# A gated mix of attention and a state-space convolution, forward and backward: a new order of work inside the channel loop

## The chip, the cores and the metric

The kernel runs on one core of one Trainium2 chip. The metric is the device time of one execution in microseconds (us). Three runs of the kernel before took 2802.67, 2806.47 and 2811.53 us; the median is 2806.47 us. A separate execution was recorded by the hardware profiler.

## The reference

The program computes a function and all its gradients (a vector-Jacobian product with a given output gradient):

```python
x = A_x                                                     # 1 x 2048 x 576, bf16
g = sigmoid((x * gate_w).sum(-1, keepdims=True))
a = attention(x, wqkv, wo)                                  # 32 heads of 18, softmax
b = s4_convolution(x, A, B, C, log_dt) + x * Dskip          # per channel, by FFT
return g * a + (1 - g) * b
```

The convolution kernel of a channel d is `K[d, l] = Re sum_n C[d,n] exp(dt_d A[d,n] l) dt_d B[d,n]`, with 128 complex states n, over the length 2048. Its outputs are the value itself and the gradients with respect to x, the attention weights, the complex parameters A, B and C, `log_dt`, `Dskip` and `gate_w`.

## The kernel before

The program has four stages, one after the other: projections and parameter preparation; attention forward and backward (most of the time); the channel loop, which does the convolution and its gradients; and a last stage with the weight gradients and the output projections. The change lies in the channel loop alone, between about 2147 and 2630 us of the profiled span.

The loop doesn't use an FFT. The 2048 positions are cut into 16 chunks of 128. Within a chunk the convolution is a 128 x 128 Toeplitz matrix for each channel (`T0w`), across chunks a recurrence runs over the 128 states. The 576 channels are taken in 18 blocks of 32 (`NBLK`, `CB`). A block passes through these steps; the engine that does it stands behind each:

- `load_en`: loads the table of powers of the exponential, `E1n`, in two halves h of 16 channels, 1 MB each (sync queue). `load_par`: three loads with 12 rows of parameters, `par` (sync). `load_rx`: the two input sequences, `RXn`, for a pair of blocks (sync).
- `prep_rx`: rearranges `RXn` into `RX`, channel by channel, and scales two copies (one copy and two multiplications of ScalarE; lines 598 to 600).
- `m_load`, `m_part`, `m_skw`, `m_sum`, `m_fin`: the gradient of the kernel at short lags. Shifted tokens `xs` and `gyp` are loaded (sync), 32 small matmuls make products in PSUM (TensorE), ScalarE copies them to `mst`, two stores put them into DRAM (`Md_d`), four loads read them back along the diagonals (`skw`), and `m_sum` adds them by eight matmuls into a column range of the PSUM tile `misc`. `m_fin` copies the result to `RX` and to a row of gradients (ScalarE). These rows are what the title's "short lags" are.
- `turn_e`: turns one half of `E1n` by 32 TensorE transposes, which four ScalarE copies bring to `E1e`.
- `uv`: 32 matmuls of `E1e` with `RX`, taken out of PSUM by four ScalarE operations to `UV`.
- `scan_open`, `scan`: the recurrence over chunks on VectorE, on `HG`, with the parameters `par`. The second half of block i's chunks and the first half of block i+1's are run together.
- `rw1`, `rw2`: VectorE makes the weighted states `Rw`. `casts`: ScalarE casts the states to bf16 (`hR`, `gR`) and copies two columns to `CK`.
- `k0`: ScalarE casts a parameter row (`wk`), 65 small matmuls make the kernel's first 128 lags in `misc`, ScalarE copies them (`K0c`), and a store writes them to DRAM (`Kp_d`). `t0_load`: reads them back as the Toeplitz matrices `T0w`, 1 MB; it waits for that store.
- `t0`: 32 matmuls of `T0w` with `RX` into the PSUM tile `yp`. `ybp`: 64 matmuls of `E1n` with `Rw` add to `yp`; ScalarE copies the sum to `yd`, and for each second block a store follows.
- `pairs1`, `pairs2`: VectorE multiplies pairs of states; 59 matmuls with the identity (`psum`) add them up in `misc`. `sums`: ScalarE copies them (`m4`, shown as `m`), GpSimd combines them into `SS`.

All PSUM results of `m_part`, `turn_e` and `uv` share four buffers (tag `bk`), `misc` has two tiles that alternate by block, and most other tiles have one or two buffers. The order on all five engines in this loop is written out by hand (`tc.manual_schedule`): each engine executes its instructions in the order in which the program text issues them. A load or a store is an instruction of the queue that issues it, so what it waits for also holds what stands behind it. In iteration i the loop works on block i (the end of its scan, `t0`, `ybp`, the pairs), on `i + 1` (first scan half, `k0`, `t0_load`), on `sb = i + 2` (`prep_rx`, `m_sum`, `turn_e`, `uv`, `load_par`) and on `mb = i + 3` (`m_part`, `load_en`, `m_skw`). Before the loop, `Md_d` and `skw` go through the sync queue; within it, through GpSimd's queue:

```python
Q["mdma"] = nc.gpsimd.dma_start
```

Of the kernel before, what the change touches and what calls it, by code (L numbers as in the profile page):

```python
# [11 lines left out]
BF = mybir.dt.bfloat16  # L12
# [5 lines left out]
P = 128  # L18


def build(tc, aps, dbg_aps=None, stages=("s1", "attn", "post", "s4", "final")):
    nc = tc.nc
# [6 lines left out]
    def mm(out, lhsT, rhs, start=True, stop=True, **kw):  # L29
        return nc.tensor.matmul(out, lhsT=lhsT, rhs=rhs, start=start, stop=stop, **kw)  # L30
# [31 lines left out]
    with ExitStack() as gctx:  # L62
# [27 lines left out]
        NS = NB - 1  # L90
# [11 lines left out]
        CB = 32  # L102
# [481 lines left out]
        def load_rx(xb, dma=nc.sync.dma_start):  # L584
            d0 = xb * XB
            RXn = Q["pl"].tile([P, 2 * NB, XB], BF, tag="RXn", bufs=1, name="RXn")
            dma(RXn[:, 0:NB, :], xr_d[:, :, d0:d0 + XB])
            dma(RXn[:, NB:2 * NB, :], gyr_d[:, :, d0:d0 + XB])
            RXs[xb] = [RXn, None]
# [88 lines left out]
        def load_en(b, h, dma=nc.sync.dma_start, pieces=1):  # L678
            dG = b * CB + h * GS
            En = blk(b)["En"][h] = Q["en", (2 * b + h) % 6 // 2].tile([P, GS, 2, P], BF, tag="E1n", bufs=2, name="E1n")  # L680
            n = GS // pieces

            def piece(x):
                dma(En[:, x * n:(x + 1) * n], E_d[:, dG + x * n:dG + (x + 1) * n])
            piece(0)
            return piece
# [45 lines left out]
                    t0v, t1v = [tz[x][:, m].rearrange("p (r s) c -> p r s c", r=2) for m in range(2)]  # L732
                    nc.vector.tensor_tensor(HG[:, :, k, :].rearrange("p (r s) c -> p r s c", r=2), t0v, t1v[:, ::-1], op=A.add)

        def casts(b):
            B_ = blk(b)
            HGv = B_["HG"].rearrange("p (r s) k c -> p r s k c", s=2)
            for nm, s_ in (("hR", 0), ("gR", 1)):
                B_[nm] = Q["pw"].tile([P, 2, NS, CB], BF, tag=nm, name=nm)
                nc.scalar.copy(B_[nm], HGv[:, :, s_, ::-1, :])  # L740
            B_["Rw"] = Q["pw"].tile([P, 2, 2 * NS, CB], BF, tag="Rw", name="Rw")
            nc.scalar.copy(Q["CK"][:, :, :, b * CB:(b + 1) * CB], B_["UV"][:, :, CDK:CDK + 2, :])

        def rw1(b):
            B_ = blk(b)
# [5 lines left out]
        def rw2(b):  # L751
# [2 lines left out]
            nc.vector.tensor_tensor(Rw[:, 0], wb[:, 2 * NS:], wa[:, 0:2 * NS], op=A.subtract)  # L754
            nc.vector.scalar_tensor_tensor(Rw[:, 1], wa[:, 2 * NS:], -1.0, wb[:, 0:2 * NS], op0=A.mult, op1=A.subtract)

        def k0(b):

            B_ = blk(b)
            wk = Q["pw"].tile([P, 2, CB], BF, tag="wk", bufs=2, name="wk")  # L760
            nc.scalar.copy(wk, B_["par"][:, 10:12, :])
            kps = Q["misc2"][b % 2][:, 13 * CB:14 * CB]
            mm(kps, lhsT=ident_bf[0:1, :], rhs=Q["dsk_row"][:, b * CB:(b + 1) * CB], start=True, stop=False)
            for ch in range(CB):
                for ri in range(2):
                    mm(kps[:, ch:ch + 1], lhsT=B_["En"][ch // GS][:, ch % GS, ri, :], rhs=wk[:, ri, ch:ch + 1],
                       start=False, stop=(ch == CB - 1 and ri == 1))
            K0c = Q["pw"].tile([P, CB], BF, tag="K0c", bufs=2, name="K0c")
            nc.scalar.copy(K0c, kps)
            nc.sync.dma_start(Kp_d[b, P:2 * P, :], K0c)  # L770

        def t0(b, h):
            B_ = blk(b)
            RX = RXs[b // 2][1]
            T0w = B_["T0w"]
            yp = B_["yp", h] = Q["ps"].tile([P, 2, NB, GS], F32, tag="yp", bufs=2, name="yp")
            for c_ in range(GS):
                mm(yp[:, :, :, c_].rearrange("p a b -> p (a b)"), lhsT=T0w[:, :, h * GS + c_],
                   rhs=RX[:, (b % 2) * CB + h * GS + c_, 0:2 * NB], start=(c_ == 0), stop=False)

        def ybp(b, h):
            B_ = blk(b)
            Rw, En = B_["Rw"].rearrange("p r (s k) c -> p r s k c", s=2), B_["En"].pop(h)
            yp = B_.pop(("yp", h))
            for c_ in range(GS):
                ch = h * GS + c_
                for ri in range(2):
                    mm(yp[:, :, 1:, c_], lhsT=En[:, c_, ri, :], rhs=Rw[:, ri, :, :, ch], start=False, stop=(c_ == GS - 1 and ri == 1))
            if h == 0 and b % 2 == 0:
                ydx[b // 2] = Q["pw"].tile([P, 2, NB, XB], BF, tag="yd", name="yd")  # L790
            yd = ydx[b // 2]
            o0 = (b % 2) * CB + h * GS
            nc.scalar.copy(yd[:, :, :, o0:o0 + GS], yp)
            if h == 1 and b % 2 == 1:
                x0 = (b // 2) * XB
                (act_dma if b == NBLK - 1 else nc.sync.dma_start)(yd_d.rearrange("p a b d -> p (a b) d")[:, :, x0:x0 + XB], yd.rearrange("p a b d -> p (a b) d"))
# [41 lines left out]
        def t0_load(b):  # L838
            B_ = blk(b)
            if "T0w" in B_:  # L840
                return
            T0w = B_["T0w"] = Q["pw"].tile([P, P, CB], BF, tag="T0w", bufs=1, name="T0w")
            src = bass.AP(tensor=Kp_d.tensor, offset=Kp_d[b:b + 1, 1:2, 0:1].offset, ap=[[CB, P], [1, P * CB]])
            nc.sync.dma_start(T0w.rearrange("p j c -> p (j c)"), src)
# [487 lines left out]
        if "s4" in stages:  # L1332
# [8 lines left out]
            with ExitStack() as ctx:  # L1341
# [26 lines left out]
                with tc.manual_schedule(engines={mybir.EngineType.SP}):  # L1368
                    prep_rx(0, dve_copy)
                    load_en(2, 0)  # L1370
                    k0(0)
                    t0_load(0)
                    turn_e(0, 0, 0, 4, dve_copy)
                    m_sum(0)
                    m_fin(0)
                    uv(0, 0)
                    prep_rx(1, dve_copy)
                    load_rx(1)
                    turn_e(0, 1, 0, 4, dve_copy)
                    m_part(1, 0)  # L1380
                    m_part(1, 1)
                    m_skw(1)
                    m_load(2)
                    uv(0, 1)
                    turn_e(1, 0, 0, 4, dve_copy)
                    scan_open(0)
                    scan((0, 1, KH, 0), (0, 1, KH, 1))
                    turn_e(1, 1, 0, 4)
                    m_sum(1)
                    m_fin(1)  # L1390
                    load_en(2, 1)
                    uv(1, 0)
                    m_part(2, 0)
                    m_part(2, 1)
                    m_skw(2)
                    uv(1, 1)
                    m_load(3)
                    Q["mdma"] = nc.gpsimd.dma_start
                    for i in range(NBLK):
                        nx = i + 1 < NBLK  # L1400
                        mb = i + 3 if i + 3 < NBLK else None
                        sb = i + 2 if i + 2 < NBLK else None
                        if nx:
                            scan_open(i + 1)
                            scan((i, KH, NS, None), (i + 1, 1, KH, None))
                        else:
                            scan((i, KH, NS, 0), (i, KH, NS, 1))
                        t0(i, 0)
                        t0(i, 1)
                        if nx:  # L1410
                            k0(i + 1)
                            t0_load(i + 1)
                        if sb is not None:
                            prep_rx(sb)
                            m_sum(sb)
                            m_fin(sb)
                            if sb % 2 == 1 and sb + 1 < NBLK:
                                load_rx((sb + 1) // 2)
                            turn_e(sb, 0, 0, 4)
                            uv(sb, 0)  # L1420
                        casts(i)
                        rw1(i)
                        rw2(i)
                        if mb is not None:
                            m_part(mb, 0)
                            m_part(mb, 1)
                            if mb + 1 < NBLK:
                                m_load(mb + 1)
                        if sb is not None:
                            load_par(sb)  # L1430
                            turn_e(sb, 1, 0, 4)
                            uv(sb, 1)
                        ybp(i, 0)
                        if mb is not None:
                            load_en(mb, 0)
                        ybp(i, 1)
                        if mb is not None:
                            load_en(mb, 1)
                            m_skw(mb)
                        pairs1(i)  # L1440
                        pairs2(i)
                        sums(i)
                        BK.pop(i)

# [297 lines left out]
```

## Time and profile before

| | |
|---|---|
| median of three runs | 2806.47 us (2802.67 to 2811.53) |
| the profiled execution's own time | 2811.18 us |
| its span in the profile | 2809.5 us |
| granted TensorE clock, mean over the span | 0.945 |
| first scan of the loop (line 708, iteration 0) | 2147.72 us |
| scan of iteration 1 | 2169.41 us |
| scan of iteration 2 | 2197.57 us |
| last of these (iteration 16) | 2591.9 us |
| DMA issues per iteration | sync queue 10 to 11, GpSimd's queue 6 |

The profile names engines PE (TensorE matmul), PEld (TensorE weight load), DVE (VectorE), ACT (ScalarE), POOL (GpSimd) and SP (the sync queue; SPq is its issuing of DMAs). A row of waits says which engine's instruction at which line stood idle until which other work ended, with the total in us, the number of times and the longest. A row of the timeline gives the start in us, the duration, the engine, the line and the operation with output and inputs; in square brackets stands the idle time before it and what ended it. Line 30 is the helper that issues every matmul, so matmuls are told apart by their tiles. "DMA share" is the sum of the durations of all DMA packets over the time of 16 engines; it can exceed 1, since packets overlap.

### The profile page before, as it was taken

The numbers are of one execution on the slowest core, as the hardware profiler recorded it, in microseconds if no ns is written. First come the engines' busy times: TensorE is split into PE (matmuls) and PEld (weight loads), VectorE is DVE, ScalarE is ACT, GpSimd is POOL, SyncE is SP. The second block draws the span as 40 slices with busy tenths as digits, with TensorE's granted clock in tenths as the row PEclk, the third lists the DMA queues.
The fourth block names the chain that finished last, engine by engine and source line by source line (L and its number), as shares of the span: only waits on it lengthen the run. The fifth ranks groups of instructions, "written<-read, shape, count | busy, mean of one in ns | idle before, by whom it ended". The sixth has DMA issues, their size and how long they took to land. (4 is left out here: it accounts for less than half of the span.)

```text
span 2809.5 us, 70096 instructions
## 1 busy us (share of the span) xinstructions
PE 2473.9 (88%) x27411; PEld 1180.0 (42%) x27411; DVE 2301.7 (82%) x4141; ACT 2356.0 (84%) x2744; POOL 1790.9 (64%) x2757
## 2 busy tenths in 40 slices
PE   8898989999889899998998989988877888888789
PEld 4433333333333333333333333333326787878557
DVE  4649999999989989999999989998866877787945
ACT  5479999999999999999999999999845777777111
POOL 0278878887888888788888888878111444443110
PEclk9879999999999999999999999999858888988899
DMA  7637899889889988977988998896698787875996
GB/s 222 179 94 160 153 173 174 161 156 189 159 161 171 168 162 164 178 161 156 186 156 159 173 168 154 164 178 140 128 201 216 198 220 205 221 204 154 251 247 143
DMA packets 1249559, 492.00 MB, mean 175 GB/s; under 512 B 1163205, under 2 KB 1216566, under 8 KB 1240522
## 3 DMA queue, kind: packets, MB, share of 16 engines
q1 hardware_dynamic: 1207466, 402.18, 71.1%
q0 software_dynamic: 28400, 72.58, 10.1%
q10 hardware_dynamic: 13360, 12.75, 1.6%
q8 instruction: 215, 3.52, 0.5%
q14 instruction: 118, 0.97, 0.1%
HBM read 146.86 MB, written 98.52 MB: 87 GB/s over the span
## 5 line engine op out<-in xcount | busy, mean ns | idle before, releaser
L1311 DVE TENSOR_TENSOR ds<-ps_P,PT 128x512 bf16<-128x512 f32 x2048 | 1312.1, 683 | 127.4 <-PE ps_P L30 87.8
L1306 ACT ACTIVATE eb<-ps_P 128x1024 bf16<-128x1024 f32 x1024 | 1101.0, 1075 | 40.0 <-PE ps_P L30 39.9
L1301 ACT ACTIVATE PT<-ps_P 128x1024 bf16<-128x1024 f32 x1024 | 1106.1, 1081 | 25.8 <-PE ps_P L30 24.7
L30 PE MATMUL ps_P<-dOaT,VaT_g 32*128 32x512 bf16 x2048 | 582.3, 390 | 29.5 <-DVE ds L1311 14.5
L502 POOL TENSOR_TENSOR et<-eG,eT 128x448 f32<-128x448 f32 x576 | 542.2, 961 | 10.7
L30 PE MATMUL ps_P<-QaT_g,KaT_g 32*128 32x512 bf16 x2048 | 404.9, 387 | 137.9 <-ACT PT L1301 124.4
L30 PE MATMUL ps_P<-KaT_g,QaT_g 32*128 32x512 bf16 x2048 | 408.3, 391 | 1.2 <-ACT eb L1306 0.6
L30 PEld LDWEIGHTS <-KaT_g 32*128 32x128 bf16 x2048 | 147.7, 91 | 467.4 <-issue 452.0
L502 POOL TENSOR_TENSOR Eo<-et,et 128x448 bf16<-128x448 f32 x288 | 326.8, 1135 | 20.8
L30 PEld LDWEIGHTS <-QaT_g 32*128 32x128 bf16 x2048 | 116.5, 91 | 287.0 <-issue 264.7
L30 PE MATMUL accV<-eb,dOa 128*32 128x512 bf16 x2048 | 186.8, 398 | 27.5 <-ACT eb L1306 27.3
L30 PE MATMUL accO<-PT,Vtok_g 128*32 128x512 bf16 x2048 | 207.7, 395 | 0.1
L30 PE MATMUL accK<-dsT,Qtok_g 128*32 128x256 bf16 x4096 | 164.0, 282 | 17.0 <-DMA dsT<-ds 15.2
L30 PE MATMUL accQ<-ds,Ktok_g 128*32 128x512 bf16 x2048 | 161.2, 393 | 2.1 <-DVE dvacc L1069 2.0
L30 PEld LDWEIGHTS <-Vtok_g 128*32 128x32 bf16 x2048 | 52.8, 93 | 223.1 <-issue 223.1
L835 POOL TENSOR_TENSOR SS<-m 128x96 f32<-128x96 f32 x18 | 100.0, 5557 | 69.4 <-ACT m L833 69.4
L1020 DVE COPY dsT<-turn_p 128x1024 bf16<-128x1024 bf16 (+1 forms) x216 | 139.1, 644 | 2.1 <-PE turn_p L1015 2.1
L1015 PE MATMUL turn_p<-ident_bf,ds 128*128 128x128 bf16 x1664 | 134.6, 224 | 1.6 <-DVE gb L1087 0.8
L30 PE MATMUL uvp<-RX,E1e 128*128 128x64 bf16 x1152 | 94.3, 260 | 40.9 <-ACT E1e L666 37.8
L666 ACT COPY E1e<-etp 128x1024 bf16<-128x1024 bf16 x132 | 127.3, 1124 | 1.5 <-PE etp L665 1.5
L502 POOL TENSOR_TENSOR et<-eT 128x32 f32<-128x32 f32 (+3 forms) x288 | 115.9, 422 | 11.4
L30 PEld LDWEIGHTS <-Qtok_g 128*32 128x32 bf16 x4096 | 88.3, 97 | 81.6 <-issue 59.8
(270 smaller groups left out, 3754.6 us busy)
## 6 DMA issues: line engine op xcount, KB each, us to landing
E_d<-Eo POOLq DMA_DIRECT2D x144, 256.0 KB, 3.4
E1n<-E_d SPq DMA_DIRECT2D x32, 1024.0 KB
xs<-xb_d SPq DMA_DIRECT2D x18, 1024.0 KB
T0w<-Kp_d SPq DMA_DIRECT2D x18, 1024.0 KB
Md_d<-mst POOLq DMA_DIRECT2D x30, 288.0 KB, 7.6
dsT<-ds SPq DMA_TRANSPOSE x512
dqkv_d<-dtk POOLq DMA_DIRECT2D x96, 72.0 KB, 4.4
KaT_g<-QKV_d SPq DMA_DIRECT2D x32, 128.0 KB
```

What stands on the lines that cost most here:

```text
L30: return nc.tensor.matmul(out, lhsT=lhsT, rhs=rhs, start=start, stop=stop, **kw)
L502: nc.gpsimd.tensor_tensor(out, a, b, op=op)
L666: copy(E_[:, 4 * q:4 * q + 4], pt_)
L835: nc.gpsimd.tensor_tensor(o_[:, :, 0], m4[:, :, 0], m4[:, :, 3], op=A.subtract)
L1015: nc.tensor.transpose(pt_[:, x, qb, :], t_[:, qb * P:(qb + 1) * P], ident_bf)
L1020: (nc.scalar.copy if NTOT <= now[0] < NTOT + OFF else nc.vector.tensor_copy)(o_(), pt_[:, x:x + n])
L1301: nc.scalar.activation(U["PT"][i, j // 2], ps, ACT.Exp)
L1306: nc.scalar.activation(e, ps, ACT.Exp)
L1311: nc.vector.tensor_tensor(U["ds"][i][:, j, :], ps, U["PT"][i, j // 2][:, j % 2, :], op=A.mult)
```

## The change

The loop's order within an iteration is rewritten. Three helpers are split so that their parts can stand apart: `casts` into `cast1` (called once for `hR`, once for `gR`), `rw2_open` and a bare copy to `CK`; `k0` into `wk_cast`, `k0` and `k0_out`; `ybp` into the matmuls and `yd_out`. `m_sum` and `m_part` now begin TensorE's iteration; `k0` follows the first `turn_e`; `t0` follows the first `uv`; the second `uv` stands between the two halves of `ybp`. `prep_rx` is done for block `mb`, one iteration earlier than before, beside the second half of `ybp`, with `prep_rx(2)` and `wk_cast(1)` ahead of the loop. `wk_cast` comes at the end of the iteration before its use. VectorE's order is as it was. The line that sends `Md_d` and `skw` to GpSimd's queue is gone, so these six DMAs stay on the sync queue in the loop.

```diff
-        def casts(b):
+        def cast1(b, nm, s_):
             B_ = blk(b)
             HGv = B_["HG"].rearrange("p (r s) k c -> p r s k c", s=2)
-            for nm, s_ in (("hR", 0), ("gR", 1)):
-                B_[nm] = Q["pw"].tile([P, 2, NS, CB], BF, tag=nm, name=nm)
-                nc.scalar.copy(B_[nm], HGv[:, :, s_, ::-1, :])
-            B_["Rw"] = Q["pw"].tile([P, 2, 2 * NS, CB], BF, tag="Rw", name="Rw")
-            nc.scalar.copy(Q["CK"][:, :, :, b * CB:(b + 1) * CB], B_["UV"][:, :, CDK:CDK + 2, :])
+            B_[nm] = Q["pw"].tile([P, 2, NS, CB], BF, tag=nm, name=nm)
+            nc.scalar.copy(B_[nm], HGv[:, :, s_, ::-1, :])
+
+        def rw2_open(b):
+            blk(b)["Rw"] = Q["pw"].tile([P, 2, 2 * NS, CB], BF, tag="Rw", name="Rw")
...
+        def wk_cast(b):
+            wk = blk(b)["wk"] = Q["pw"].tile([P, 2, CB], BF, tag="wk", bufs=2, name="wk")
+            nc.scalar.copy(wk, blk(b)["par"][:, 10:12, :])
+
         def k0(b):
...
-            wk = Q["pw"].tile([P, 2, CB], BF, tag="wk", bufs=2, name="wk")
-            nc.scalar.copy(wk, B_["par"][:, 10:12, :])
+            wk = B_["wk"]
...
+        def k0_out(b):
+            kps = Q["misc2"][b % 2][:, 13 * CB:14 * CB]
             K0c = Q["pw"].tile([P, CB], BF, tag="K0c", bufs=2, name="K0c")
...
+            B_["yp", h] = yp
+
+        def yd_out(b, h):
+            yp = blk(b).pop(("yp", h))
...
                 with tc.manual_schedule(engines={mybir.EngineType.SP}):
                     prep_rx(0, dve_copy)
                     load_en(2, 0)
+                    wk_cast(0)
                     k0(0)
+                    k0_out(0)
...
                     m_load(3)
-                    Q["mdma"] = nc.gpsimd.dma_start
+                    prep_rx(2)
+                    wk_cast(1)
                     for i in range(NBLK):
...
-                        t0(i, 0)
-                        t0(i, 1)
-                        if nx:
-                            k0(i + 1)
-                            t0_load(i + 1)
+                        rw1(i)
+                        rw2_open(i)
+                        rw2(i)
                         if sb is not None:
-                            prep_rx(sb)
                             m_sum(sb)
                             m_fin(sb)
-                            if sb % 2 == 1 and sb + 1 < NBLK:
-                                load_rx((sb + 1) // 2)
-                            turn_e(sb, 0, 0, 4)
-                            uv(sb, 0)
-                        casts(i)
-                        rw1(i)
-                        rw2(i)
                         if mb is not None:
                             m_part(mb, 0)
                             m_part(mb, 1)
                             if mb + 1 < NBLK:
                                 m_load(mb + 1)
                         if sb is not None:
+                            turn_e(sb, 0, 0, 4)
+                        if nx:
+                            k0(i + 1)
+                        if nx:
+                            k0_out(i + 1)
+                        cast1(i, "hR", 0)
+                        nc.scalar.copy(Q["CK"][:, :, :, i * CB:(i + 1) * CB], BK[i]["UV"][:, :, CDK:CDK + 2, :])
+                        if sb is not None:
+                            uv(sb, 0)
+                        t0(i, 0)
+                        t0(i, 1)
+                        if nx:
+                            t0_load(i + 1)
+                        cast1(i, "gR", 1)
+                        if mb is not None:
+                            m_skw(mb)
+                        if sb is not None:
+                            turn_e(sb, 1, 0, 4)
                             load_par(sb)
-                            turn_e(sb, 1, 0, 4)
-                            uv(sb, 1)
                         ybp(i, 0)
                         if mb is not None:
                             load_en(mb, 0)
+                        if sb is not None:
+                            uv(sb, 1)
                         ybp(i, 1)
                         if mb is not None:
                             load_en(mb, 1)
-                            m_skw(mb)
+                            prep_rx(mb)
+                            if mb % 2 == 1 and mb + 1 < NBLK:
+                                load_rx((mb + 1) // 2)
+                        yd_out(i, 0)
+                        yd_out(i, 1)
                         pairs1(i)
                         pairs2(i)
+                        if sb is not None:
+                            wk_cast(sb)
                         sums(i)
                         BK.pop(i)
```

## The prediction

> **What bounds the kernel now.** I read the page's busy table first, then the channel loop alone (eleven of its iterations, 2197.57 to 2507.40 us), then who waits there, then TensorE's order of time in one iteration.
>
> ```profile
> ## 1 busy us (share of the span) xinstructions
> PE 2473.9 (88%) x27411; PEld 1180.0 (42%) x27411; DVE 2301.7 (82%) x4141; ACT 2356.0 (84%) x2744; POOL 1790.9 (64%) x2757
> ```
>
> No engine is full over the span; the diff touches only the channel loop, so that stretch decides.
>
> ```profile
> core 0: us, PE busy (x) PEld busy (x) DVE busy (x) ACT busy (x) POOL busy (x), PEclk, DMA share, GB/s
> 2197.57:2507.40 309.83, 271.82 (x4256) 242.96 (x4254) 239.69 (x572) 225.15 (x351) 138.91 (x88) 0.88 0.81 211
> ```
>
> 309.83 us are eleven iterations: 28.17 us each, of which VectorE is busy 21.8, ScalarE 20.5 and the DMA engines 0.81 x 28.17 = 22.8 us. Nothing is saturated, so waits set the period:
>
> ```profile
> DVE HG L708 <- ACT UV L702: 35.8, 11, 3.3
> ACT K0c L769 <- PE misc L30: 33.7, 11, 3.1
> ACT m L833 <- PE misc L30: 30.7, 11, 2.8
> PE uvp L30 <- ACT E1e L666: 26.1, 55, 1.3
> DVE tz L727 <- DMA par<-par_d: 19.6, 11, 3.5
> ```
>
> Each is us in total, times, longest. ScalarE idles for TensorE (K0c, m), TensorE for ScalarE (uvp), VectorE for ScalarE (HG). The sync queue waits as well:
>
> ```profile
> SPq L684 <- PE yp L30: 84.9, 22, 5.3
> SPq L844 <- DMA Kp_d<-K0c: 31.9, 11, 4.0
> ```
>
> ```profile
> 2344.26 2.12 PE L30 MATMUL yp<-RX,T0w 128*128 128x32 bf16 x32
> 2346.31 0.18 PE L30 MATMUL misc<-dsk_row,ident_bf 1*128 1x32 bf16 x1
> 2346.43 1.75 PE L30 MATMUL misc<-wk,E1n 128*128 128x1 bf16 x64
> ...
> 2350.05 3.26 PE L665 MATMUL etp<-ident_bf,E1n 128*128 128x128 bf16 x32
> 2353.72 0.43 PE L30 MATMUL uvp<-RX,E1e 128*128 128x64 bf16 x4 [0.41 <-ACT E1e L666]
> 2354.63 1.31 PE L30 MATMUL uvp<-RX,E1e 128*128 128x64 bf16 x16 [0.47 <-ACT E1e L666]
> ...
> 2357.23 2.15 PE L30 MATMUL psM<-xs,gyp 128*32 128x128 bf16 x32
> 2359.31 1.07 PE L665 MATMUL etp<-ident_bf,E1n 128*128 128x128 bf16 x16
> ...
> 2365.68 3.62 PE L30 MATMUL yp<-Rw,E1n 128*128 128x30 bf16 x64
> 2369.12 3.47 PE L30 MATMUL misc<-pq,ident_bf 128*128 128x128 bf16 x59
> ```
>
> The order is serial. From K0c (2348.22) to the last UV (2366.93) ScalarE works 18.7 us without a gap and paces TensorE: 32 transposes take 3.26 us, though 16 run in 1.07. Then TensorE does ybp, psum, t0 and k0 in a row, 9.4 us to the next K0c, with ScalarE nearly idle. 18.7 + 9.4 = 28.1.
>
> **What the Trainium skill says.** "Trace Analysis", Identifying the Most-Contended Engine: matmul busy is no measure of how full TensorE is; agreed, see 3.26 against 2 x 1.07. "TensorE: Matmul & The Clock Gate", What's actually happening: idleness halves the clock; the loop was granted 0.88, about one half-speed spell per iteration. "DMA: Bandwidth & Descriptors", Issuing engines are not separate DMA queues: another issuer saves only issue time on the same 16 engines; one skw issue takes 0.61 us on POOL and 0.58 on SP before the loop, so the move changes order, not bytes. Same page, Anatomy of one DMA: a wait is held by the issuing sequencer, so it blocks what is queued behind; agreed, E1n's issues hold SP 84.9 us above.
>
> **The change, part by part.** Nothing is added or removed but order, so I take each resource's own work per iteration and ask what keeps it from that.
>
> *TensorE* (differences of starts, unpaced): m_sum 1.06, m_part 2.08, turn_e 2 x 2.16, k0 1.87, t0 2.05, ybp 3.44, psum 3.31 = 18.1; uv twice, 1.77 each where nothing paced it (32 in the prologue, 2144.96 to 2146.73), 2.3 paced: 21.7 to 22.7. New wait: m_sum now directly follows psum and writes the tile that ScalarE's m copy (0.49) reads; the like wait on K0c (0.18) costs 0.28 now, so 0.6 here. Behind it stand m_part and turn_e. TensorE: 22.3 to 23.3.
>
> *ScalarE*: prep_rx 3.94, m_fin 0.31, two E1e sets 7.25, two UV sets 4.0, casts and CK 2.0, mst 0.96, yd, m, wk, K0c 1.7: 20.2. Each consumer now has another block of TensorE work between producer and itself (k0 after turn_e, ybp after the second), so the 26.1 us of uvp waits mostly go; prep_rx lies under ybp and psum. If that cover failed, its 3.94 us would land on the period.
>
> *VectorE*: scan 10.5, rw1 and rw2 6.9, pairs 4.4: 21.8. Its loop: Rw ready 17.4 us after the scan's start, ybp's first half 1.7, uv 1.8 to 2.3, last eviction 0.4: the next scan may start at 21.3 to 21.8. So uv's new place hides the 3.3 us HG wait.
>
> *Sync queue*: it now carries 2 Md_d stores and 4 skw loads that POOL issued, 16 DMAs per iteration for 10. Issue time: about 5.4 us now by its rows, + 2 x 0.44 + 4 x 0.58 (the prologue's SP rows) = 8.6 us, no bound. Each issue also waits for the DMA eight before it; En0 then waits for T0w to land, near its ybp wait anyway. The order matters: xs, gyp, Kp_d store, T0w, skw, par, E1n. Kp_d is a small store queued behind xs, T0w cannot start until it lands, and skw, par and E1n stand behind T0w. So the DMA engines run dry once per iteration. Work 22.8 us, or 21.0 if, in the packets, moments with more than one per engine count once; plus Kp_d's turnaround, 1.95 us at its shortest (2348.43 to 2350.38). Period by DMA: 23.0 to 24.8. What is late next is par, 0.2 MB behind T0w and skw, for which VectorE's scan and now also ScalarE's wk cast wait; behind wk stand m and then m_sum. E1n's first half, due at the next turn_e, has uv, half ybp, psum, m_sum and m_part, 10 us, for 1 MB, which takes 5.0 us even at the loop's mean 211 GB/s.
>
> *POOL*: loses six issues, 4.0 us; not on a path.
>
> The four bounds are 22.7 (TensorE's middle), 20.2, 21.8 and 23.9. The largest is DMA; a denser period queues more, so I take the upper half: 24.4, keeping 22.3 and 27 as ends.
>
> *Once*: in iteration 0 m_sum and m_part come first and need skw and gyp of the prologue. gyp was issued at 2150.76; the previous took 7.2 us (2135.76 to TensorE's release at 2142.92), so 2157.9. From there m_part, turn_e, k0, uv, t0, turn_e, half ybp, uv, eviction: 16.6 us, next scan at 2174.5 against 2169.4: +5.1. *Last*: iteration 15 has no mb work, 22.3. From scan 16 on (2591.9) VectorE sets the end in both.
>
> Sum from the first scan to scan 16: 26.8 + 14 x 24.4 + 22.3 = 390.7 against 444.2 (2147.7 to 2591.9): -53.5. The profiled execution took 2811.2 (span 2809.5, 1.7 around it): 2757.7. The median of runs, 2806.5, lies 4.7 lower: 2753.0.
>
> **Rivals.**
> 1. Likeliest, the DMA order bounds, period 23.0 to 25.5: -73 to -38, 2733 to 2768.
> 2. Transfers hidden, TensorE or VectorE bounds, period 22.0 to 23.0: 2719 to 2733. For: 14% of the loop has idle DMA engines, and T0w has most of an iteration until its t0. Against: 22.8 of 23 us.
> 3. par late every time, VectorE and ScalarE both held, 25.5 to 27.9: 2768 to 2802. For: par already costs 19.6 us in eleven iterations with T0w some 10 us ahead of it.
> 4. Slower. One mechanism: Kp_d's turnaround, serial on the one queue. Before, the wait averages 31.9/11 = 2.9 and reaches 4.0 us. It decides from 28.2 - 22.8 = 5.4 us on; at 6.5 the period is 29.3, +20 with iteration 0: 2826. For: xs, yd and RXn all precede it now. Against: the queueing is already in the 22.8.
> 5. No change: the loop re-balances to within 8 us, 2798 to 2815.
>
> **How the numbers follow.** Chances 0.54, 0.13, 0.21, 0.08, 0.04. 0.3% (8 us) is about what can be told from no change. The prediction is 2753, the likeliest's own range 2733 to 2768. Down to 2727 takes half of rival 2, up to 2787 most of rival 3: about 8 in 10. Faster: 1, 2 and nearly all of 3, 0.87; within 0.3%: 0.05; slower: 0.08.
>
> **What would show it.** Right: VectorE's scan starts about 24 us apart; the waits of K0c, uvp and HG nearly gone; a wait on DMA par, and Kp_d before T0w in SP's waits; granted clock above 0.88; DMA share over 0.9. Wrong: a period near 22 with no par wait (rival 2), T0w or par waits of 4 us and more (3, 4), TensorE waiting for E1n, or ScalarE's prep_rx holding TensorE.

## The result and the profile after

The changed kernel takes 2761.8 us (median of four runs, 2756.15 to 2764.32) against 2809.0 us for the kernel before (four runs). The ratio is 0.9832, with a 95% interval of 0.9805 to 0.9858: faster by 1.7%, 47 us. The profiled execution took 2764.32 us, with a span of 2762.6 us, 46.9 us less than the one before.

The page's first part of the changed kernel shows the same work in a shorter span. TensorE is busy for 43.8 us less, with as many matmuls as before; GpSimd for 75.6 us less, with 90 instructions fewer, the six DMAs of fifteen iterations:

```profile
## 1 busy us (share of the span) xinstructions
PE 2430.1 (88%) x27411; PEld 1159.8 (42%) x27411; DVE 2301.0 (83%) x4141; ACT 2360.2 (85%) x2744; POOL 1715.3 (62%) x2667
```

The useful cut is at the starts of the scan (line 708 on VectorE). All times are us of one profiled execution of each kernel:

| stretch | before | after | difference | forecast |
|---|---|---|---|---|
| start to the loop's first scan | 2147.72 | 2141.51 | -6.2 | 0 |
| iteration 0 | 21.7 | 26.2 | +4.5 | +5.1 |
| iterations 1 to 14, mean | 28.2 | 25.2 | -3.0 each | -3.8 each |
| iteration 15 | 27.4 | 23.8 | -3.6 | -5 |
| first scan to the scan of iteration 16 | 444.2 | 403.0 | -41.2 | -53.5 |
| from there to the end | 217.6 | 218.1 | +0.5 | 0 |

The mean of iterations 1 to 14 hides a spread: they take 28.0 to 28.5 us before, 22.7 to 28.7 us after. The first row isn't the change: what this adds ahead of the loop (`prep_rx(2)`, `wk_cast(1)`) begins on ScalarE at 2141.37 us, when the first scan is about to start, and over the 13 profiled kernels of this study the first scan starts anywhere between 2132.9 and 2152.6 us. The loop's own length, from the first scan to that of iteration 16, is free of this scatter and is used below beside the medians.

Busy time in twelve iterations after, in the same columns as before:

```profile
core 0: us, PE busy (x) PEld busy (x) DVE busy (x) ACT busy (x) POOL busy (x), PEclk, DMA share, GB/s
2191.16:2495.60 304.44, 267.25 (x4657) 250.36 (x4655) 261.55 (x625) 249.55 (x385) 92.70 (x24) 0.93 0.89 236
```

An iteration is now 25.37 us long in this stretch. VectorE is busy for 21.8 of it, as before. The DMA share rose from 0.81 to 0.89, the granted clock from 0.88 to 0.93. The waits in that stretch (us in total, times, longest):

```profile
DVE tz L727 <- DMA par<-par_d: 33.7, 12, 5.3
...
PEld misc L30 <- ACT m L843: 18.5, 12, 2.6
...
PE yp L30 <- DVE Rw L754: 11.1, 9, 1.9
PE yp L30 <- DVE Rw L755: 9.1, 11, 0.9
...
DVE HG L708 <- ACT UV L702: 6.4, 6, 1.5
...
ACT K0c L775 <- PE misc L30: 0.4, 1, 0.4
```

The old list is turned over (it was of eleven iterations, this is of twelve). The exchange between TensorE and ScalarE is nearly gone: K0c's wait fell from 33.7 to 0.4 us, HG's from 35.8 to 6.4, and the matmuls' wait for E1e (26.1) is no longer there. In their place VectorE waits 2.8 us per iteration for `par`; the late scan makes `Rw` late, for which TensorE waits 1.7 us; and `m_sum` waits 1.5 us for ScalarE's copy m. VectorE's account of an iteration nearly closes: 21.8 us of work, 2.8 of waiting for `par` and 0.5 for HG's UV are 25.1 of the 25.4 us. TensorE's order of time in an iteration shows both the gain and the two gaps that are left:

```profile
2424.01 1.06 PE L30 MATMUL misc<-sel,skw 128*128 128x8 f32 x8 [1.12 <-ACT m L843]
2425.00 2.12 PE L30 MATMUL psM<-xs,gyp 128*32 128x128 bf16 x32
2427.06 1.96 PE L665 MATMUL etp<-ident_bf,E1n 128*128 128x128 bf16 x32
...
2430.69 1.95 PE L30 MATMUL uvp<-RX,E1e 128*128 128x64 bf16 x32
2432.44 2.07 PE L30 MATMUL yp<-RX,T0w 128*128 128x32 bf16 x32
2434.35 1.95 PE L665 MATMUL etp<-ident_bf,E1n 128*128 128x128 bf16 x32
2437.30 0.21 PE L30 MATMUL yp<-Rw,E1n 128*128 128x30 bf16 x1 [1.00 <-DVE Rw L754]
```

`uv` runs in 1.95 us without a gap. The 32 transposes take 1.96 us here and took 3.26 before, but that is no sign of ScalarE's pace: no wait stood between them. TensorE ran most of that stretch at half speed (a granted clock of 0.5), as the mean granted clock (PEclk) of the two stretches shows, 0.56 before and 1.00 after:

```profile
2350.05:2353.31 3.26, 3.26 (x34) 2.99 (x33) 3.26 (x8) 3.26 (x7) 3.26 (x2) 0.56 0.65 226
```

```profile
2427.06:2429.02 1.96, 1.96 (x37) 1.86 (x33) 1.96 (x9) 1.79 (x3) 1.96 (x1) 1.00 1.32 189
```

The same holds for the first 32 transposes of all iterations 1 to 14 before (clock 0.50 to 0.58). After, where a spell of half speed falls on them, they take up to 3.4 us.

On the sync queue one wait is far longer than the others:

```profile
SPq L854 <- DMA Kp_d<-K0c: 78.7, 12, 7.8
```

That is 6.6 us per iteration in which the queue stands at T0w's load until the small store of `K0c` has landed; before, it was 2.9. The queue's order of time says what the store is behind and who stands behind T0w:

```profile
2404.88 0.55 SPq L608 DMA_DIRECT2D xs<-xb_d  x1
2405.49 0.73 SPq L609 DMA_DIRECT2D gyp<-gyb_d  x1
2406.31 0.40 SPq L776 DMA_DIRECT2D Kp_d<-K0c  x1
2414.54 0.32 SPq L854 DMA_DIRECT2D T0w<-Kp_d  x1
2414.95 2.49 SPq L635 DMA_DIRECT2D skw<-Md_d  x4
2417.54 0.96 SPq L675 DMA_DIRECT2D par<-par_d  x2
2418.54 1.49 SPq L676 DMA_DIRECT2D par<-par_d  x1
```

From 2406.71 to 2414.54 nothing is issued. Then `par` goes out 3 us after T0w, behind the four `skw` loads, and VectorE's scan, ready at 2418.60, has to wait for it:

```profile
2421.40 0.42 DVE L727 TENSOR_TENSOR tz<-HG,par 128x256 f32<-128x256 f32 x1 [2.24 <-DMA par<-par_d]
```

### The profile page after: what moved, and what is told of

It is laid out like the page before. It is cut to its first block, busy times and chain, and to the rows that moved or that the text cites. A ratio compares the mean times of both kernels' runs of the same rounds, so it can differ in the third digit from the quotient of the medians.

```text
span 2762.6 us, 70109 instructions
## 1 busy us (share of the span) xinstructions
PE 2430.1 (88%) x27411; PEld 1159.8 (42%) x27411; DVE 2301.0 (83%) x4141; ACT 2360.2 (85%) x2744; POOL 1715.3 (62%) x2667
## 5 line engine op out<-in xcount | busy, mean ns | idle before, releaser
L845 POOL TENSOR_TENSOR SS<-m 128x96 f32<-128x96 f32 x18 | 91.0, 5053 | 340.6 <-ACT m L843 285.9
L727 DVE TENSOR_TENSOR tz<-HG,par 128x256 f32<-128x256 f32 (+1 forms) x245 | 92.6, 412 | 39.0 <-DMA par<-par_d 39.0
```

The lines of the kernel that those rows point to most:

```text
L727: nc.vector.tensor_tensor(tz[x], HG[:, :, k - 1, :].unsqueeze(1).to_broadcast([P, 2, n, CB]), ZZ, op=A.mult)
L845: nc.gpsimd.tensor_tensor(o_[:, :, 0], m4[:, :, 0], m4[:, :, 3], op=A.subtract)
```

## The experiments

Two questions were open. Does this chain on the sync queue (Kp_d, T0w, skw, par: theory A) set the new period, or TensorE's wait for m (rival B), or the DMA engines' bytes (rival C)? And what do the change's two parts, order and queue, each bring? Every kernel was timed beside the kernel before; ratios are to that. "Loop" is the length from the first scan to that of iteration 16: 444.2 us before, 403.0 after. It is read from one profiled execution of each kernel, so a few us between two rows mean little unless the medians agree.

| kernel | median us | ratio, 95% interval | loop us | mean of iterations 1 to 14 |
|---|---|---|---|---|
| the change | 2761.8 | 0.9832, 0.9805 to 0.9858 | 403.0 | 25.2 |
| T0w of old rows | 2742.3 | 0.9767, 0.9739 to 0.9794 | 381.4 | 23.5 |
| par first | 2748.7 | 0.9779, 0.9741 to 0.9817 | 384.0 | 23.8 |
| Kp_d first | 2764.7 | 0.9843, 0.9814 to 0.9871 | 398.2 | 24.7 |
| m_part first | 2773.2 | 0.9878, 0.9839 to 0.9916 | 404.7 | 25.2 |
| order alone | 2740.2 | 0.9770, 0.9740 to 0.9799 | 383.8 | 23.9 |
| queue alone | 2831.8 | 1.0084, 1.0055 to 1.0114 | 468.9 | 30.0 |
| par and m_part first | 2741.1 | 0.9763, 0.9738 to 0.9788 | 380.8 | 23.4 |
| par, skw and m_part first | 2743.9 | 0.9793, 0.9758 to 0.9828 | 375.7 | 23.2 |
| order alone, m_part first | 2749.0 | 0.9782, 0.9753 to 0.9810 | 377.8 | 23.3 |
| order alone, par and m_part first | 2730.9 | 0.9734, 0.9710 to 0.9759 | 370.3 | 22.8 |
| the same without xs | 2722.7 | 0.9686, 0.9665 to 0.9707 | 360.0 | 21.9 |

**T0w of old rows.** The load's wait is taken away by giving it other data:

```diff
-            src = bass.AP(tensor=Kp_d.tensor, offset=Kp_d[b:b + 1, 1:2, 0:1].offset, ap=[[CB, P], [1, P * CB]])
+            src = bass.AP(tensor=Kp_d.tensor, offset=Kp_d[max(b - 1, 0):max(b - 1, 0) + 1, 1:2, 0:1].offset, ap=[[CB, P], [1, P * CB]])
```

> T0w is loaded from the rows of the block before, so the load has no store of its own iteration to wait for (the Toeplitz matrices, and with them the outputs that use them, are those of a wrong block). Theory A (the queue's chain Kp_d store, T0w, skw, par sets the period): the sync queue's 6.6 us wait before T0w falls to about 2 us or less, VectorE's 2.8 us wait for par goes, the period falls from 25.2 to about 23.5 us, 2761.8 - 24 = 2738 us. Rival B (TensorE and ScalarE set it, through m_sum's wait for m): at most 5 us gained, 2757 us or more. Rival C (the DMA engines' bytes set it): no gain, the wait shows up at E1n or skw instead.

Measured: the loop is 21.6 us shorter, and the period is the 23.5 us that theory A gave. The queue's 78.7 us wait for Kp_d is gone, TensorE's `t0` takes its place as what T0w is held by (its matmuls still read the one buffer of T0w), 2.8 us per iteration, and the wait for par falls from 33.7 to 11.9 us rather than to nothing. Waits of the sync queue and of VectorE:

```profile
SPq L854 <- PE yp L30: 33.6, 12, 3.1
```

```profile
DVE tz L727 <- DMA par<-par_d: 11.9, 12, 2.7
```

So the store's landing is worth at least 1.7 us per iteration. Rivals B and C had no room for this gain.

**par first.** `load_par` moves from behind `skw` to ahead of T0w:

```diff
                         t0(i, 0)
                         t0(i, 1)
+                        if sb is not None:
+                            load_par(sb)
                         if nx:
                             t0_load(i + 1)
...
                             turn_e(sb, 1, 0, 4)
-                            load_par(sb)
```

> par is issued before T0w and skw instead of after them. Theory A, with par as the link that costs: VectorE's wait for par goes (2.8 us per iteration), period about 23.8 us, 2742 us. If the link that costs is not par but E1n or T0w behind it: same time, with waits there. Rival B: 2757 us or more. Rival C: no gain.

Measured: 384.0 us, period 23.8 as expected; the median is 13 us lower, with intervals that just overlap. VectorE has hardly a wait for par left (0.7 us, twice); it waits for ScalarE's UV instead, and TensorE for skw and E1n a little:

```profile
DVE HG L708 <- ACT UV L702: 22.3, 12, 3.6
...
PE misc L30 <- DMA skw<-Md_d: 7.5, 7, 2.5
...
PEld L665 <- DMA E1n<-E_d: 4.2, 7, 1.1
```

The queue still waits 61.4 us in twelve iterations for Kp_d. What costs most, then, is not that wait itself but that `par` stood behind it.

**Kp_d first.** The load of `xs` and `gyp` goes behind the store:

```diff
                             m_part(mb, 1)
-                            if mb + 1 < NBLK:
-                                m_load(mb + 1)
...
                             k0_out(i + 1)
+                        if mb is not None and mb + 1 < NBLK:
+                            m_load(mb + 1)
```

> The load of xs and gyp is issued after the Kp_d store instead of before it. Theory A: the queue's wait before T0w falls from 6.6 to about 2.5 us, as the store no longer stands behind 1.1 MB; T0w, skw and par come 4 us earlier, the wait for par goes, about 2740 us. Rival B: 2757 us or more. Rival C: no gain, since the bytes are the same.

Measured: the first half came, the gain did not. The wait before T0w fell to 8.8 us in twelve iterations, but the loop is only 4.8 us shorter and the median not lower. The waits of the sync queue show why:

```profile
SPq L675 <- DMA xs<-xb_d: 18.3, 12, 2.5
...
SPq L684 <- DMA T0w<-Kp_d: 12.7, 12, 2.3
...
SPq L854 <- DMA Kp_d<-K0c: 8.8, 8, 2.3
```

In these traces a DMA of the sync queue has the same semaphore as the one eight places before it, and `par`, which reads nothing of xs, waits for xs to land. In the changed kernel too a load of `par` stands eight places behind xs, but there xs has landed while the queue stood at T0w. Here the queue reaches `par` sooner, and xs, now one place later, is still on its way: 1.5 us of waiting per iteration. So part of the wait moved from T0w to `par`, and VectorE still waits 26.1 us for `par` (33.7 before the move). This fits theory A, with `par` as the link; its expected size for this edit was wrong.

**m_part first.** TensorE's `m_part` before `m_sum`, ScalarE's `m_fin` after the `mst` copies:

```diff
-                        if sb is not None:
-                            m_sum(sb)
-                            m_fin(sb)
                         if mb is not None:
                             m_part(mb, 0)
                             m_part(mb, 1)
+                        if sb is not None:
+                            m_sum(sb)
+                            m_fin(sb)
+                        if mb is not None:
```

> TensorE does m_part before m_sum, so that the 2.1 us of m_part cover ScalarE's copy m, for which m_sum waits 1.5 us per iteration. Rival B (this wait sets the period): 15 x 1.4 = 21 us gained, 2741 us. Theory A: the 1.5 us come back as TensorE's wait for Rw, which follows par: at most 5 us gained, 2757 us or more.

Measured: no gain (404.7 against 403.0 us; the median is 11 us higher, with intervals that just overlap). The wait for m is gone from TensorE's list, and the waits for Rw grew from 20.2 to 29.9 us in twelve iterations:

```profile
PE yp L30 <- DVE Rw L754: 19.6, 12, 2.1
...
PE yp L30 <- DVE Rw L755: 10.3, 12, 0.9
```

That is what theory A said, and it rules out rival B: TensorE merely waits elsewhere while VectorE's scan comes late.

**Order alone and queue alone.** Each part of the change by itself. The first puts one line back into the changed kernel; the second takes the same line out of the kernel before:

```diff
                     wk_cast(1)
+                    Q["mdma"] = nc.gpsimd.dma_start
                     for i in range(NBLK):
```

```diff
                     m_load(3)
-                    Q["mdma"] = nc.gpsimd.dma_start
                     for i in range(NBLK):
```

> The new order with Md_d and skw on GpSimd's queue, as before the change. Theory A (Kp_d, T0w, skw, par in one queue set the period): with skw out of the queue par is issued 2.5 us earlier behind T0w, VectorE's wait for par falls from 2.8 to under 1 us, the loop from its first scan to the last from 403.0 to about 385 us, 2743 us in all. Rival D (the rows on GpSimd come too late, behind its two SS operations of about 8 us): m_sum waits for skw, 2762 us or more.

> The old order with Md_d and skw on the sync queue. Theory A: in the old order par is issued ahead of these rows, and the period is set by the exchange between TensorE and ScalarE, so the move is worth little: the loop stays within 8 us of 444 us, 2800 to 2818. If the queue were the gain: 2790 us or less.

Measured: the order alone brings 67 us (2807.7 to 2740.2), the loop 60.4. Its wait for par:

```profile
DVE tz L727 <- DMA par<-par_d: 12.0, 9, 2.5
```

A third of the changed kernel's, and TensorE hardly waits for skw (1.3 us in twelve iterations): rival D fell. Which of the moves within the order brings how much of the 60 us was not tested. The granted clock doesn't explain it: before, two iterations with 3.4 us at half speed (7 and 11) take 28.2 us, and one with 10.2 (4) takes 28.4. The queue alone costs 24 us (2807.7 to 2831.8; loop +24.7). That was outside the expected 2800 to 2818. The old order has the Md_d stores ahead of xs and par, and the skw loads behind E1n, and both are felt (the last line is of the sync queue):

```profile
DVE tz L727 <- DMA par<-par_d: 43.3, 12, 4.7
...
PE misc L30 <- DMA skw<-Md_d: 36.6, 13, 5.9
```

```profile
SPq L622 <- ACT mst L621: 89.3, 12, 9.7
```

The queue stands 7.4 us per iteration at the first Md_d store, waiting for ScalarE's copy, with xs and par behind it; GpSimd's queue took that wait before. In both orders the move to the sync queue costs about the same: 19.2 us of loop in the new one, 24.7 in the old one. The change is the sum of a gain of 60 us and a loss of 19.

**par and m_part first; skw too.** Both edits from above together on the sync queue, and then `m_skw(mb)` also ahead of `t0_load`, behind `load_par`:

> par ahead of T0w, and m_part ahead of m_sum. Theory A: with par out of the way (the loop at 384.0 us) TensorE is 92% busy and its wait for m, 2.9 us per iteration by both its rows or 1.8 at the least, is what remains, so m_part ahead of m_sum, worth nothing alone, is now worth 10 to 20 us: the loop 365 to 374 us, 2728 to 2738 us. Rival C (the DMA engines, already 0.95 busy): no further gain, 2745 us or more.

> As the one before, with skw too ahead of T0w, so that only T0w and what follows stand behind the Kp_d store. Theory A: skw's late arrival at m_sum (9.6 us in twelve iterations with par first) goes as well: 2725 to 2735 us. Rival C: the wait moves to E1n, which is behind T0w still: same as the one before or worse.

Measured: 380.8 and 375.7 us of loop, 2741.1 and 2743.9 us, with intervals that overlap: moving skw can't be told from nothing by the times. Together par and m_part first gained 3 us of loop over par first alone, not the 10 to 20 expected. TensorE's wait for m is gone, but E1n comes late in its place (in the first of the two kernels; a second row, of the matmuls, shows the same waits again):

```profile
PEld L665 <- DMA E1n<-E_d: 11.8, 7, 3.4
```

In each of the two kernels six of the iterations 1 to 14 take 21.8 to 21.9 us, VectorE's own work, and others up to 27 us. A late load fits rival C, but E1n stands behind T0w, and T0w behind the Kp_d store (the queue still waits 54.0 us for it in the first of the two), so the order on the queue would do the same: this pair doesn't decide.

**On GpSimd's queue: m_part first, and par and m_part first.**

> The new order with Md_d and skw on GpSimd's queue, and m_part ahead of m_sum. TensorE waits 1.5 us per iteration for m in the new order alone (18.3 us in twelve). If that wait is on the path once the queue is out of the way: 14 x 1.4 = 20 us off 2740, 2720 to 2728 us. If par is what binds by then (12.0 us in twelve): no more than 5 us gained, 2735 or more.

> The same with par ahead of T0w as well: no wait for par, none for m. VectorE's own work, 21.8 us, is the floor of an iteration, 27 + 15 x 22 = 357 us for the loop against 383.8 with the new order alone, 2715 to 2722 us. If the DMA engines bind (0.94 busy at 23.9 us, 22.5 us of work): E1n's waits appear, the period stays at 23 us or above, 2730 us or more.

Measured: m_part first alone shortens the profiled loop from 383.8 to 377.8 us, but its median is 9 us higher, with overlapping intervals, and the profiled executions themselves lie 14 us apart (2735.7 and 2750.1); this one is inconclusive. With par first as well the kernel takes 2730.9 us, 0.9734 of before (0.9710 to 0.9759): the fastest here of those that leave nothing out, 1% below the change. Over the new order alone (0.9740 to 0.9799) the intervals still overlap. The loop is 370.3 us, not the 357 of VectorE's floor. The waits for par and E1n do not appear; skw's is 6.0 us in twelve iterations, HG's 13.4 us. The stretch of these twelve:

```profile
2192.99:2467.23 274.24, 261.45 (x4667) 245.76 (x4665) 260.57 (x625) 248.79 (x385) 138.21 (x96) 0.96 0.98 258
```

VectorE is busy for 260.57 of 274.24 us, and the DMA share is 0.98. What is above VectorE's work isn't spread evenly. Seven of the iterations 1 to 14 take 21.8 to 21.9 us, with TensorE's clock at 1.00 throughout; the other seven take 22.9 to 24.9 us, and each has a spell of 3.4 to 6.8 us at half speed. Iterations 3 and 4:

```profile
2214.84:2236.69 21.85, 21.00 (x392) 19.67 (x390) 21.71 (x54) 20.66 (x33) 10.27 (x6) 1.00 0.98 263
2236.69:2261.57 24.88, 23.47 (x396) 22.09 (x394) 21.71 (x54) 21.04 (x33) 12.72 (x11) 0.86 1.01 257
```

In four of the seven (4, 7, 10 and 13) `m_sum` waits for skw, 0.7 to 1.6 us, just before the spell; in the other three TensorE waits only for Rw, 0.9 us, as it does in iterations without a spell.

**The same without xs.** From block 4 on the shifted tokens are not loaded:

```diff
                             if mb + 1 < NBLK:
-                                m_load(mb + 1)
+                                xss[mb + 1] = xss[mb]
```

> As the one before, but the shifted tokens xs and gyp are loaded no more after block 3: all later blocks use those of block 3 (their short-lag gradient is wrong), which takes 1.15 MB, about a fifth of the DMA work, out of each iteration. If the DMA engines bind there: VectorE's floor of 21.8 us is reached, E1n's and HG's waits gone, 10 to 20 us faster than with xs. If not: the same time within 4 us.

```profile
2185.55:2447.80 262.25, 251.85 (x4660) 236.06 (x4658) 260.59 (x626) 247.67 (x385) 138.26 (x96) 1.00 0.78 219
```

Measured: every iteration from the second to the fifteenth takes 21.8 to 21.9 us, VectorE is busy for 260.59 of 262.25 us, and the waits for HG and skw are gone. The loop is 10 us shorter than with xs and the median 8, at and just under the low end of the 10 to 20 expected. So VectorE's 21.8 us is the floor, and loading xs is what kept the kernel above it. How isn't decided: by the bytes, by xs standing ahead of Kp_d and skw, or through the clock, which is 1.00 here in all fourteen iterations. This run removes all three at once.

## Why the prediction was right, and where its size was off

*What bounded the kernel before.* That the hand-written order made ScalarE and TensorE take turns was right: the order alone took 60.4 us out of the loop, and of the waits named for it K0c's and uvp's fell to nearly nothing and HG's to less than a third (39.1 to 10.8 us in twelve iterations), while VectorE's 21.8 us and ScalarE's work stayed. ScalarE's 18.7 us without a gap carry that reading. The other sign, "32 transposes take 3.26 us, though 16 run in 1.07", was misread: it is TensorE's half speed there. The clock rose as said, to 0.93.

*What bounds it after.* The prediction took the DMA order, Kp_d's store ahead of T0w with par and skw behind it, as the largest of four bounds. The period is set on that chain: with the store's landing taken away it falls by 1.7 us, with par ahead of it by 1.4 us, and with TensorE's wait for m taken away by nothing. But the form of the bound was another than the sum had it. The sum added a turnaround to the DMA engines' work; measured, the chain makes `par` late, and the period is VectorE's 21.8 us with its waits. The prediction had named par as what is late next, and gave it no term. Two of the signs came out the other way: the DMA share is 0.89, a little short of "over 0.9", and the queue's wait before T0w, 6.6 us, is above the 4 us that were to speak for rivals 3 and 4.

*The failing term.* The forecast was 390.7 us of loop, 403.0 was measured. Of the 12.3 us, 11.3 are 14 iterations of 25.2 us for 24.4; iteration 15 adds 1.5 (23.8 for 22.3) and iteration 0 gives back 0.6. The mis-sized step is "Kp_d's turnaround, 1.95 us at its shortest". From the store's issue to T0w's, as it was counted there, it measured 7.0 us on the average of twelve iterations, 6.6 of them the queue's wait; with xs and gyp behind the store that wait fell to 0.7, so it queued behind their 1.1 MB. (1.95 wasn't the shortest before either: iteration 11 has 1.44, and the mean was 3.3.) I had counted that queueing within the 22.8 us of work and taken only the dead time on top. The two do overlap for the most part: had all 7.0 us come on top of 22.8, the period would have been 29.8 and the kernel slower. That the forecast came within 0.8 us of the period is thus in part luck: the turnaround was put too low, and adding it to the work was wrong. In the version with par and m_part first on GpSimd's queue T0w still comes 6.2 us after the store, and half of the iterations take 21.8 to 21.9 us. The experiments show which part was missing: par stands behind that wait, and is due before T0w is.

*The queue's move, "order, not bytes".* That was right in kind, but I gave it no price of its own: it went into the DMA bound and the sum doesn't show it. It costs 19 us in the new order. The prediction took over that another issuer saves only issue time; with issue times alike, the measured 19 and 25 us say that here it saved waits as well.

*m_sum's wait for m* was put at 0.6 us and measured 1.5, since `prep_rx`, two `yd` copies and the cast of par's rows stand ahead of m on ScalarE. It cost nothing here; it is covered by the wait for Rw.

*Iteration 0* was forecast by its late gyp: +5.1 us. It measured +4.5, and the trace shows the wait:

```profile
2149.88 2.15 PE L30 MATMUL psM<-xs,gyp 128*32 128x128 bf16 x32 [5.29 <-DMA gyp<-gyb_d]
```

*The rivals.* Rival 3, par late every time, came in a mild form: 2.8 us per iteration, and a period of 25.2, just under the 25.5 from which it was counted. Rival 2, transfers hidden and a period of 22 to 23, didn't occur, but is what the best version reaches (22.8 us), and its floor, VectorE's 21.8 us, was measured in the run without xs. The medians moved by 47 us, 6 less than the forecast 53.5, though the loop fell short by 12. In the profiled executions 6.2 of the 46.9 us come from the part before the loop, which the change doesn't touch: that is scatter, and this much of the agreement is luck.

## What to carry to other kernels

When engines take turns in a hand-written order, add up each engine's own work, put another block of one engine's work between a producer and its consumer on the other, and expect the period to fall to the next bound rather than to the largest engine's sum. On an in-order queue, sort the issues by when their data is due and by what they must wait for: a small store followed by the load that reads it back holds all that is behind it, so loads that wait for nothing belong ahead of the pair. A second queue can be worth more than its issue time, because it takes over waits: 19 and 25 us here.

## What the runs showed that was not expected

- The same six DMAs per iteration cost 19 to 25 us more on the sync queue than on GpSimd's, though their bytes are the same and issuing one skw load costs 0.59 us on the one and 0.61 on the other: what counts is whose loads wait behind them.
- An edit that took a wait of the queue away from T0w (Kp_d first) brought part of it back at `par`, through the reuse of DMA semaphores.
- The granted clock rose as the loop grew shorter: 0.88 before, 0.93 after, 0.96 in the best version, 1.00 in the run without xs. TensorE's busy share doesn't tell it apart (88% both before and after, 95% and 96% in the last two), and the longest gap between its recorded matmuls in twelve iterations before is 1.3 us, so the idleness to which the prediction put half speed down comes in short pieces at most. What brings a spell of half speed on was not tested.
- In the version with par and m_part first on GpSimd's queue every one of iterations 1 to 14 that is longer than VectorE's own work has such a spell. A long operation in a trace is worth a look at the clock of its stretch before it is put down to a wait.
